# A GEGLU feed-forward kernel: the last float32r product of its down stage as seven block products of 256 columns

## The chip, the cores and the metric

The kernel runs on one core of a Trainium2 chip. The time is the device time of one execution in microseconds; of three executions of the kernel before, the median was 270.98 us (270.94 to 271.31). Five engines work side by side, each with its own queue of instructions: TensorE (PE in the profile; its weight loads are the row PEld), VectorE (DVE), ScalarE (ACT), GpSimd (POOL) and SyncE (SP). SP, ACT and POOL also start transfers (DMAs). Engines wait for each other through semaphores.

## The reference

The input x has 32 x 32 tokens of width 1024, taken as 1024 rows; the weights are w_gate and w_up (1024 x 3584) and w_down (3584 x 1024), all bfloat16.

```
def _gelu(x):
    return jax.nn.gelu(x, approximate=True)

def reference(x, w_gate, w_up, w_down):
    return (_gelu(x @ w_gate) * (x @ w_up)) @ w_down
```

## The kernel before

**Recording and planning.** Every instruction is recorded with `pr.add` (line 58), which works out what it must wait for from the 256-byte pieces of memory that it reads and writes. An instruction has a wished time `at`; `finish` (line 184) sorts each engine's instructions by it, TensorE excepted, which keeps the order of recording, and `emit` (line 205) issues them, so all instructions of the profile carry line 216. Before that, `arrange` (line 124) replaces the wished times in a window `lo` to `hi` by a plan: it walks through the program with a cost for each instruction (`cost`, line 91) and, on each engine but TensorE and SP, takes the instruction that can start first, urgent ones ahead; `SHIFT` (line 830) moves the urgency of single instructions. The window before is 39 to `base` (about 180 us), so the plan covers the gate and up stage. The order in the down stage is written out by hand through the wished times.

**Gate and up stage (to about 180 us).** 28 slabs of 128 columns of the hidden layer are computed into `hT`, stored transposed: `hT[:, m, n]` has the 128 hidden units of slab m on the partitions and 1024 tokens n in the columns, in bfloat16. From slab pair 3 on (`SECOND`), one of the products of each pair is itself taken as seven block products of 256 columns (`inner`, line 572). In this stage POOL makes part of the weight sums, and one sum of each of nine pairs (`sums_w`, line 468) is made by a ScalarE copy and an adding transfer: a DMA issued by POOL with `accum_op=ADD`, which adds its source to what stands at its destination.

**Down stage.** The product of `hT` (3584 x 1024 tokens) with the down weights `wd` (3584 x 1024 columns) is split in two along tokens (i), hidden units (j) and columns, and the eight half-size products are replaced by seven. Products 1 and 2 are plain bfloat16; products 7, 5, 6, 3 and 4 (in this order) are float32r products of sums of activations and sums of weights. Each of the seven is a `sweep` (line 741): 14 slabs deep, 4 tiles of 128 tokens, 512 columns, so 56 matrix products. VectorE makes the sums in pieces of 1024 columns (`prep7` to `prep4`, lines 774 to 792): activation sums into 20 slots of `S`, weight sums into 16 slots of `T2r`. A slot is used again when TensorE has read it. ScalarE makes plain float32r copies where an operand is no sum (`cs`). PSUM has eight banks, four for each of two groups, `PA` and `PB`; ScalarE copies a finished group into the other where two results begin alike.

Product 4, the last sweep, is the one that the change replaces. Its stationary operand is the activations h11 (slabs 14 to 27, tokens 512 to 1023), copied to float32r by ScalarE (`cs(1, k)`); its moving operand is the weight sum `ws(2, k)`; it is added on top of the sums that stand in `PA`. Two lines set it up, and its results leave through `done4` (line 798), alternately over VectorE and ScalarE:

```
tt(bank(PA[t]), bank(PA[t]), p7[t], ADD, begin[3] + 2.9 + 0.1 * t)
tt(late[:, 0, t, :], bank(PA[t]), p5[t], ADD, begin[3] + 2.9 + 0.1 * t)
...
sweep(4, PA, False, lambda k, t: S[:, c_at(1, k), t * P:(t + 1) * P], one_w(2), done4, prep4)
```

The second of these lines makes four output tiles while product 3 starts, and SP stores them (`out_dma`, line 736). After product 4 TensorE does a bfloat16 rest that was left over from product 2: 14 products of 384 and 14 of 128 columns (line 818), each piece copied out and stored by SP. The rest's PSUM banks are filled from `p1` by ScalarE.

Of the kernel before, what the change touches and what calls it, by code (L numbers as in the profile page):

```python
# [6 lines left out]
P = 128  # L7
# [12 lines left out]
class _Program:  # L20
# [70 lines left out]
    def cost(self, op):  # L91
        name, args, _ = op.call
        ins = [a for a in args[1:] if hasattr(a, "tensor")]
        n = math.prod(args[0].shape[1:])
        if op.eng == "pe":
            wide = ins and ins[-1].dtype == F32R
            step = max(n / 2400 + (0.0133 if wide else 0.0026), 0.112 if wide else 0.056)
            return step, step + 0.165
        if op.sem:
            if name != "dma_start":  # L100
                return 1.25, 6.0
            size = math.prod(args[0].shape) * WIDTH[args[0].dtype] / 1e6
            if op.eng == "pool":
                return (1.5, 3.8 + size / 0.19) if op.call[2] else (1.0, 3.1 + size / 0.3)
# [118 lines left out]
def bass_standalone__geglu_ffn__sampling_kernel(  # L223
# [21 lines left out]
    with ExitStack() as es:  # L245
        def sb(name, shape, dtype):
            return es.enter_context(nc.sbuf_tensor(name, shape, dtype))

        hT = sb("hT", [P, FM, N], BF16)
        arena = sb("arena", [P, 28672], BF16)  # L250
        S = sb("S", [P, 20, 512], F32R)
        T = sb("T", [P, 8, 4, 2, P], F32R)
# [12 lines left out]
        pr.alias = {tqr.name: (tmp[:, :, :].tensor.name, 8192), p1r.name: (p1[:, :].tensor.name, 0)}  # L265
# [25 lines left out]
        def tt(out, a, b, op, at, eng="dve", after=()):  # L291
            return pr.add(eng, "tensor_tensor", out, a, b, op, at=at, after=after)
# [4 lines left out]
        def dma(eng, out, a, at, name, after=()):  # L297
            return pr.add(eng, "dma_start", out, a, at=at, dma=name, after=after)
# [413 lines left out]
        def wb(i, j, k): return wd[i][j][:, k:k + 2, :]  # L712


        s_at = lambda b, k: 2 * ((b * 7 + k // 2) % 10) + k % 2
        t_at = lambda b, k: 2 * ((b * 7 + k // 2) % 8) + k % 2
        c_at = lambda b, k: 2 + 2 * ((b * 7 + k // 2) % 3) + k % 2
        hs = lambda b, k: S[:, s_at(b, k):s_at(b, k) + 2, :]
        hsf = lambda b, k: Sf[:, s_at(b, k):s_at(b, k) + 2, :]
        ws = lambda b, k: T2r[:, t_at(b, k):t_at(b, k) + 2, :]  # L720
        wsf = lambda b, k: T2f[:, t_at(b, k):t_at(b, k) + 2, :]
        cs = lambda b, k: S[:, c_at(b, k):c_at(b, k) + 2, :]
# [4 lines left out]
        late = arena[:, 0:6144].rearrange("p (o t n) -> p o t n", o=3, n=512)  # L727
        F, H = 0.2266, 0.216
        begin = {}
        now = base  # L730
        for n in (1, 2, 7, 5, 6, 3, 4):
            begin[n] = now
            now += (3 if n == 2 else 4) * NK * (H if n < 3 else F)
        end = now + NK * H

        def out_dma(i, t, j, src):
            dma("sp", out_r[:, 4 * i + t, j * 512:(j + 1) * 512], src, end, "out")

        EDGE = 4

        def sweep(n, banks, start, stat, mov, done, prep=None):


            held = 2 if n == 7 else 3
            steps = [(t, k) for k in range(EDGE) for t in range(4) if t != held] + [(held, k) for k in range(EDGE)]
            steps += [(t, k) for k in range(EDGE, NK - EDGE) for t in range(4)]
            steps += [(t, k) for t in range(4) for k in range(NK - EDGE, NK)]
            if n < 3:
                steps = [(t, k) for t in range(5 - n) for k in range(NK)]
            made = set()  # L750
            for i, (t, k) in enumerate(steps):
                if prep and k // 2 not in made:
                    made.add(k // 2)
                    prep(k)
                mm(banks[t], stat(k, t), mov(k), start and k == 0, k == NK - 1, add=not start)
                if k == NK - 1:
                    done(t, begin[n] + (i + 1) * (H if n < 3 else F))
# [20 lines left out]
        def prep5(k):  # L778
            tt(hs(1, k), hb(1, 0, k), hb(1, 1, k), ADD, clock + V * (14 + k))
            tt(ws(1, k), wb(0, 1, k), wb(0, 0, k), SUB, clock + V * (15 + k))  # L780

        def prep6(k):
            tt(hs(2, k), hsf(1, k), hb(0, 0, k), SUB, clock + V * (28 + k))
            tt(ws(2, k), wb(1, 1, k), wsf(1, k), SUB, clock + V * (29 + k))

        def prep3(k):
            tt(hs(2, k), hb(0, 1, k), hsf(2, k), SUB, max(begin[6] + 4 * F * (k + 3), clock + V * (42 + k / 2)))
            act(cs(0, k), wb(1, 1, k), COPY, begin[3] + 4 * F * (k - 5))

        def prep4(k):  # L790
            tt(ws(2, k), wb(1, 0, k), wsf(2, k), SUB, begin[3] + 3.5 + 4 * F * k)
            act(cs(1, k), hb(1, 1, k), COPY, begin[4] + 4 * F * (k - 5))

        def done3(t, at):
            tt(late[:, 1, t, :], bank(PB[t]), p5[t], ADD, at)
            out_dma(0, t, 1, late[:, 1, t, :])

        def done4(t, at):
            if t % 2 == 0:
                pr.add("dve", "tensor_copy", late[:, 2, t, :], bank(PA[t]), at=at)  # L800
            else:
                act(late[:, 2, t, :], bank(PA[t]), COPY, at)
            out_dma(1, t, 0, late[:, 2, t, :])

        one_t = lambda b: (lambda k, t: S[:, s_at(b, k), t * P:(t + 1) * P])
        one_w = lambda b: (lambda k: T2r[:, t_at(b, k), :])
        sweep(7, PA, True, one_t(0), one_w(0), lambda t, at: act(p7[t], bank(PA[t]), COPY, at), prep7)
        sweep(5, PA, True, one_t(1), one_w(1), lambda t, at: act(p5[t], bank(PA[t]), COPY, at), prep5)
        sweep(6, PB, False, one_t(2), one_w(2), lambda t, at: act(bank(PA[t]), bank(PB[t]), COPY, at), prep6)
# [4 lines left out]
        sweep(3, PB, False, one_t(2), lambda k: S[:, c_at(0, k), :], done3, prep3)  # L814
        sweep(4, PA, False, lambda k, t: S[:, c_at(1, k), t * P:(t + 1) * P], one_w(2), done4, prep4)


        pieces = ((PB[0], 0, 384), (PB[1], 384, 512))
        for b, c0, c1 in pieces:
            act(ps[:, b, 0:c1 - c0], p1[:, c0:c1], COPY, begin[4] + 6)  # L820
        for b, c0, c1 in pieces:
            for k in range(NK):
                mm(b, ht(0, 1, k, 3), wd[1][0][:, k, c0:c1], False, k == NK - 1, add=True)
            if c0 == 0:
                act(o11[:, 3, c0:c1], ps[:, b, 0:c1 - c0], COPY, end)
            else:
                pr.add("dve", "tensor_copy", o11[:, 3, c0:c1], ps[:, b, 0:c1 - c0], at=end)
            dma("sp", out_r[:, 3, c0:c1], o11[:, 3, c0:c1], end, "out")

        SHIFT = {0: {16: 0.4, 22: -1.3},  # L830
                 2: {11: 0.2},
                 11: {7: -0.5},
                 12: {21: 1.8},
                 "steady": {22: 1.7}}
# [5 lines left out]
_INS = ['x', 'w_gate', 'w_up', 'w_down']  # L840
_OUTS = [((32, 32, 1024), 'bfloat16')]
# [23 lines left out]
```

## Time and profile before

| what | value |
|---|---|
| median of three executions | 270.98 us |
| the profiled execution's own time | 270.95 us |
| its span, first to last instruction | 269.3 us |
| TensorE busy | 266.6 us (99%) |
| VectorE busy | 229.4 us (85%) |
| ScalarE busy | 137.4 us (51%) |
| POOL busy | 88.8 us (33%) |
| product 3 starts, product 4 starts, rest starts | 238.82, 251.51, 264.21 us |
| granted TensorE clock | 1.00 throughout |

Times in the profile count from the span's start; around the span lie another 1.65 us of the execution. A row of a group names the source line, the engine, the operation, the written and read tiles with their shape and how often it occurred, then the busy time, the mean duration in ns and the idle time before it with what ended it. A row of a timeline has the start, the time to the end of the last instruction merged into it, and the count. A matrix product's duration includes its drain, which overlaps the next product; the pace is read from the starts. TensorE is busy all the time, so the other engines' busy shares matter only where TensorE would have to wait for them, and the last stores matter because the execution ends when they have landed.

### The profile page before, as it was taken

The numbers are of one execution on the slowest core, as the hardware profiler recorded it, in microseconds if no ns is written. First come the engines' busy times: TensorE is split into PE (matmuls) and PEld (weight loads), VectorE is DVE, ScalarE is ACT, GpSimd is POOL, SyncE is SP. The second block draws the span as 40 slices with busy tenths as digits, with TensorE's granted clock in tenths as the row PEclk, the third lists the DMA queues.
The fourth block names the chain that finished last, engine by engine and source line by source line (L and its number), as shares of the span: only waits on it lengthen the run. The fifth ranks groups of instructions, "written<-read, shape, count | busy, mean of one in ns | idle before, by whom it ended". The sixth has DMA issues, their size and how long they took to land.

```text
span 269.3 us, 3654 instructions
## 1 busy us (share of the span) xinstructions
PE 266.6 (99%) x1272; PEld 193.5 (72%) x1272; DVE 229.4 (85%) x301; ACT 137.4 (51%) x243; POOL 88.8 (33%) x69
## 2 busy tenths in 40 slices
PE   8999999999999999999999999999999999999997
PEld 3444448888888888888586867764458888888884
DVE  1338999999999999999999999599976999999921
ACT  1339877666676576656464755521220305067452
POOL 1000019499798999995524330000000000000000
DMA  6999955995999999998930700492010000002102
GB/s 193 221 349 234 252 157 65 163 242 68 185 217 202 251 224 233 231 251 196 281 127 0 253 22 1 125 353 69 2 39 19 0 0 2 0 1 78 58 22 97
DMA packets 63746, 36.94 MB, mean 137 GB/s; under 512 B 8944, under 2 KB 63728, under 8 KB 63728
## 3 DMA queue, kind: packets, MB, share of 16 engines
q1 hardware_dynamic: 42496, 25.04, 33.0%
q0 software_dynamic: 18720, 9.44, 28.2%
q10 hardware_dynamic: 2512, 2.23, 3.1%
q8 instruction: 10, 0.16, 0.2%
q14 instruction: 8, 0.07, 0.1%
HBM read 23.33 MB, written 2.10 MB: 94 GB/s over the span
## 4 chain that ended last, share of the span: by engine, by line
PE 99%; DVE 0%; issue 0%
PE ps L216 99%; DVE o L216 0%
## 5 line engine op out<-in xcount | busy, mean ns | idle before, releaser
L216 PE MATMUL ps<-S,T 128*128 128x512 f32 (+1 forms) x516 | 120.1, 383 | 0.0
L216 PEld LDWEIGHTS ps<-S,T 128*128 128x128 f32 x516 | 94.6, 188 | 18.6 <-DMA T<-arena 0.2
L216 ACT ACTIVATE tmp<-ps 128x512 f32<-128x512 f32 (+1 forms) x75 | 36.3, 505 | 38.7 <-PE ps L216 37.5
L216 DVE TENSOR_TENSOR T<-arena,T 128x1024 fp32r<-128x1024 bf16 x42 | 54.6, 1308 | 0.1
L216 PE MATMUL ps<-T,S 128*128 128x512 f32 x224 | 51.3, 390 | 0.0
L216 PEld LDWEIGHTS ps<-T,S 128*128 128x128 f32 x224 | 42.1, 188 | 8.8
L216 POOL TENSOR_TENSOR T<-arena 128x1024 fp32r<-128x1024 bf16 x17 | 38.3, 2255 | 21.1 <-PE ps L216 19.2
L216 ACT ACTIVATE ps<-ps 128x512 f32<-128x512 f32 (+1 forms) x55 | 28.9, 537 | 32.0 <-PE ps L216 31.4
L216 PE MATMUL ps<-arena 128*128 128x512 bf16 x192 | 42.6, 381 | 0.0
L216 DVE TENSOR_TENSOR hT<-tmp,ps 128x512 bf16<-128x512 f32 x56 | 37.1, 680 | 5.0 <-PE ps L216 4.1
L216 DVE TENSOR_TENSOR tmp<-ps,tmp 128x256 f32<-128x256 f32 (+1 forms) x72 | 35.4, 522 | 5.6 <-PE ps L216 4.0
L216 PEld LDWEIGHTS ps<-arena 128*128 128x128 bf16 x192 | 17.8, 98 | 23.7 <-ACT ps L216 2.4
L216 ACT ACTIVATE tmp<-tmp 128x512 f32<-128x512 f32 x28 | 17.5, 632 | 21.7 <-DVE tmp L216 21.7
L216 PE MATMUL ps<-arena,hT 128*128 128x512 bf16 (+2 forms) x126 | 24.6, 356 | 0.0
L216 DVE TENSOR_TENSOR ps<-ps,tmp 128x512 f32<-128x512 f32 x32 | 22.2, 696 | 2.6 <-PE ps L216 2.3
L216 POOL DMA_DIRECT2D T<-arena x18 | 22.3, 1434 | 6.2 <-ACT T L216 3.4
L216 DVE TENSOR_TENSOR T<-arena 128x1024 fp32r<-128x1024 bf16 x16 | 19.0, 1220 | 4.0 <-PE ps L216 4.0
L216 PEld LDWEIGHTS ps<-arena,hT 128*128 128x128 bf16 x126 | 11.7, 98 | 12.8 <-issue 0.5
L216 POOL TENSOR_TENSOR tq<-S 128x512 fp32r<-128x512 f32 x2 | 4.2, 2090 | 38.1 <-PE ps L216 38.1
L216 DVE TENSOR_TENSOR S<-hT 128x1024 fp32r<-128x1024 bf16 x14 | 16.6, 1219 | 0.0
L216 ACT ACTIVATE ps<-hT 128x512 f32<-128x512 f32 x22 | 13.0, 596 | 4.5 <-DVE hT L216 2.4
L216 ACT ACTIVATE T<-arena 128x1024 fp32r<-128x1024 bf16 x14 | 14.8, 1059 | 0.4
(50 smaller groups left out, 200.3 us busy)
## 6 DMA issues: line engine op xcount, KB each, us to landing
T<-arena POOLq DMA_DIRECT2D x18, 512.0 KB, 6.7
arena<-in_w_down_dram SPq DMA_DIRECT2D x4, 1792.0 KB, 9.0
arena<-in_w_gate_dram SPq DMA_DIRECT2D x10, 512.0 KB, 4.0
arena<-in_w_up_dram SPq DMA_DIRECT2D x10, 512.0 KB, 5.3
out_dram<-arena SPq DMA_DIRECT2D x12, 128.0 KB, 1.7
arena<-in_w_up_dram ACTq DMA_DIRECT2D x6, 128.0 KB, 5.3
arena<-in_w_gate_dram SPq DMA_DIRECT2D x3, 256.0 KB, 5.6
arena<-in_w_up_dram SPq DMA_DIRECT2D x3, 256.0 KB, 5.9
```

The lines of the kernel that those rows point to most:

```text
L216: ins = name(eng, *args, **kw) if callable(name) else getattr(eng, name)(*args, **kw)
```

## The change

Product 4 is itself split in two along tokens, depth and columns, and computed as seven block products: each has 7 depths, 2 tiles of 128 tokens and 256 columns, 98 matrix products in all. The depth is split by even and odd slabs (h11, h12, h21, h22 of `rows` are views of `hT`).

- Activations: a11, a12 and a22 are float32r copies by ScalarE. The four sums s1 = h21 + h22, s2 = s1 - h11, s3 = h11 - h21 and s4 = h12 - s2 are made by a ScalarE copy or negation followed by an adding transfer from POOL (`plus`). s4 needs s2 first, and s2 needs s1. They lie in `wr`, memory that held the down weights wd[0][0] and wd[0][1]; a11, a12 and more lie over the front of `hT` (`hr`, `hf`).
- Weights: four sets of differences by VectorE (`sums_b`), each in a part of 5 and a part of 2 depths, 1280 and 512 columns. The last set is written over weights that an earlier block reads.
- Results: blocks that begin alike are copied between PSUM banks by ScalarE (256 columns); VectorE joins blocks with `u3` (the sum of what stood in `PA` and product 7) in 256-column additions.
- The four output tiles that were made at the start of product 3 are now made among the last block results and stored by POOL (queue name `side`) rather than SP; SP waits for both at the end.
- Slots: activation and weight sums sit at other places, four pairs of weight sums of product 5 in `spare`, a view of `tmp`; all sums of product 5 are recorded ahead of its sweep.
- `arrange` now covers the down stage too (`end + 20` in place of `base`), with another `SHIFT`, and the plan's cost of a POOL transfer has one more rate. By the order of the instructions that results, VectorE has 18 more than before, ScalarE 2 more, POOL 8 more, SP 4 fewer and TensorE 42 more; in the gate and up stage only a few neighbours on ScalarE and VectorE change places.

```
+        hr = nc.alloc_sbuf_tensor_at("hr", [P, FM, 512], F32R, offset=at_h)
+        hf = nc.alloc_sbuf_tensor_at("hf", [P, FM, 512], FP32, offset=at_h)
+        wr = nc.alloc_sbuf_tensor_at("wr", [P, 4, 7, 256], F32R, offset=at_w)
...
-            out_dma(0, t, 0, o11[:, t, :])
+            out_dma(0, t, 0, o11[:, t, :], "out" if t else "early")
...
+        def negate(o, a, at):
+            pr.add("act", "activation", o, a, COPY, at=at, scale=-1.0)
...
-        def prep4(k):
-            tt(ws(2, k), wb(1, 0, k), wsf(2, k), SUB, begin[3] + 3.5 + 4 * F * k)
-            act(cs(1, k), hb(1, 1, k), COPY, begin[4] + 4 * F * (k - 5))
...
-        for t in range(4):
-            tt(bank(PA[t]), bank(PA[t]), p7[t], ADD, begin[3] + 2.9 + 0.1 * t)
-            tt(late[:, 0, t, :], bank(PA[t]), p5[t], ADD, begin[3] + 2.9 + 0.1 * t)
-            out_dma(1, t, 1, late[:, 0, t, :])
-        sweep(4, PA, False, lambda k, t: S[:, c_at(1, k), t * P:(t + 1) * P], one_w(2), done4, prep4)
...
+        rows = [hT[:, 14 + i:28:2, 512 + r * 256:768 + r * 256] for r in range(2) for i in range(2)]
+        h11, h12, h21, h22 = rows
+        a11, a12, a22 = hr[:, 0:7, 0:256], hr[:, 7:14, 0:256], flat(8192)
+        s1, s2, s3, s4_ = (wr[:, i] for i in range(4))
+
+        def plus(o, a, name, after=()):
+            pr.add("pool", "dma_start", o, a, at=begin[6] + 6, dma=name, after=after, accum_op=ADD)
+
+        act(s1, h21, COPY, begin[6])
+        plus(s1, h22, "sa")
+        negate(s2, hT[:, 14:28:2, 512:768], begin[6] + 1)
+        plus(s2, s1.bitcast(FP32), "sb")
+        negate(s3, h21, begin[6] + 2)
+        plus(s3, h11, "sc")
+        negate(s4_, s2.bitcast(FP32), begin[6] + 4)
+        plus(s4_, h12, "sd")
+
+        u3 = p7
+        for t in range(4):
+            tt(u3[t], bank(PA[t]), p7[t], ADD, begin[3] + 2.9 + 0.1 * t)
...
+        act(a11, h11, COPY, begin[3])
+        act(a12, h12, COPY, begin[3] + 1)
+        act(a22, h22, COPY, begin[4])
...
+        def sums_b(out, p, q):
+            for k0, k1 in ((0, 5), (5, 7)):
+                tt(out(k0, k1), p(k0, k1).bitcast(FP32), q(k0, k1).bitcast(FP32), SUB, begin[3] + 6)
+        B = lambda i, c: (lambda k0, k1: b(i, c, k0, k1))
+        T1 = lambda k0, k1: hr[:, k0:k1, 256:512]
+        T2_ = lambda k0, k1: flat(6144)[:, k0:k1, :]
+        sums_b(T1, B(0, 1), B(0, 0))
+        sums_b(T2_, B(1, 1), T1)
+        sums_b(B(0, 1), B(1, 1), B(0, 1))
+
+        def block(bk, l, r, start, t):
+            for k in range(7):
+                pr.add("pe", "matmul", ps[:, bk, 0:256], l[:, k, t * P:(t + 1) * P], r(k, k + 1)[:, 0, :],
+                       start=start and k == 0, stop=k == 6, skip_group_check=not start)
+
+        for t in range(2):
+            block(q0[t], a11, B(0, 0), True, t)
+            act(q(q1[t]), q(q0[t]), COPY, begin[4])
+        for t in range(2):
+            block(q5[t], s1, T1, True, t)
+            tt(r5[2 + t], q(q5[t]), u3[2 + t][:, R], ADD, begin[4])
+            tt(r5[t], q(q5[t]), u3[t][:, R], ADD, begin[4])
+        for t in range(2):
+            block(q1[t], s2, T2_, False, t)
+            act(q(q5[t]), q(q1[t]), COPY, begin[4])
+        for t in range(2):
+            block(q0[t], a12, B(1, 0), False, t)
+            tt(done4(t)[:, L], q(q0[t]), u3[t][:, L], ADD, begin[4])
+        sums_b(B(1, 0), B(1, 0), T2_)
+        for t in range(4):
+            tt(late(t), u3[t], p5[t], ADD, begin[4], after=pr.ops["dve"][-1:])
+            out_dma(1, t, 1, late(t), "side", "pool")
+        for t in range(2):
+            block(q5[t], s3, B(0, 1), False, t)
+            tt(done4(2 + t)[:, R], q(q5[t]), r5[2 + t], ADD, begin[4])
+        for t in range(2):
+            block(q1[t], s4_, B(1, 1), False, t)
+            tt(done4(t)[:, R], q(q1[t]), r5[t], ADD, begin[4])
+            out_dma(1, t, 0, done4(t))
+        for t in range(2):
+            block(q5[t], a22, B(1, 0), False, t)
+            tt(done4(2 + t)[:, L], q(q5[t]), u3[2 + t][:, L], ADD, begin[4])
+            out_dma(1, 2 + t, 0, done4(2 + t))
...
-        pr.arrange(39, base, range(4, 9), SHIFT)
+        pr.arrange(39, end + 20, range(4, 9), SHIFT)
...
-            pr.emit(e, eng, sems, [("out", totals["out"])] if e == "sp" else ())
+            pr.emit(e, eng, sems, [(n, totals[n]) for n in ("out", "side")] if e == "sp" else ())
```

More of the change, by code (lines that the diff above doesn't have):

```diff
@@ L103, in cost @@
             if op.eng == "pool":
-                return (1.5, 3.8 + size / 0.19) if op.call[2] else (1.0, 3.1 + size / 0.3)
+                rate = 0.25 if args[0].shape[-1] > 256 else 0.19 if op.call[2] else 0.3
+                return (1.5, 3.8 + size / rate) if op.call[2] else (1.0, 3.1 + size / rate)
             return 0.62, 2.6 + size / 0.25
@@ L247, in sb @@
             return es.enter_context(nc.sbuf_tensor(name, shape, dtype))
+        at_h = (nc.sbuf_base + 31) // 32 * 32
         hT = sb("hT", [P, FM, N], BF16)
+        at_w = (nc.sbuf_base + 31) // 32 * 32
+        assert at_w == at_h + 57344
         arena = sb("arena", [P, 28672], BF16)
@@ L264, in bass_standalone__geglu_ffn__sampling_kernel @@
         p1r = nc.alloc_sbuf_tensor_at("pq", [P, 2, 2, P], F32R, offset=at_p1)
-        pr.alias = {tqr.name: (tmp[:, :, :].tensor.name, 8192), p1r.name: (p1[:, :].tensor.name, 0)}
+        hr = nc.alloc_sbuf_tensor_at("hr", [P, FM, 512], F32R, offset=at_h)
+        hf = nc.alloc_sbuf_tensor_at("hf", [P, FM, 512], FP32, offset=at_h)
+        wr = nc.alloc_sbuf_tensor_at("wr", [P, 4, 7, 256], F32R, offset=at_w)
+        pr.alias = {hr.name: (hT[:, :, :].tensor.name, 0), hf.name: (hT[:, :, :].tensor.name, 0), wr.name: (arena[:, :].tensor.name, 0), tqr.name: (tmp[:, :, :].tensor.name, 8192), p1r.name: (p1[:, :].tensor.name, 0)}
         ps = es.enter_context(nc.psum_tensor("ps", [P, 8, 512], FP32))
@@ L712, in wb, with wsn @@
         def wb(i, j, k): return wd[i][j][:, k:k + 2, :]
-        s_at = lambda b, k: 2 * ((b * 7 + k // 2) % 10) + k % 2
-        t_at = lambda b, k: 2 * ((b * 7 + k // 2) % 8) + k % 2
-        c_at = lambda b, k: 2 + 2 * ((b * 7 + k // 2) % 3) + k % 2
+        s_at = lambda b, k: 2 * ((0, 7, 14, 14 if k < 8 else 7)[b] + k // 2) % 20 + k % 2
+        c_at = lambda k: 2 * (8, 9, 0)[k // 2 % 3] + k % 2
         hs = lambda b, k: S[:, s_at(b, k):s_at(b, k) + 2, :]
         hsf = lambda b, k: Sf[:, s_at(b, k):s_at(b, k) + 2, :]
-        ws = lambda b, k: T2r[:, t_at(b, k):t_at(b, k) + 2, :]
-        wsf = lambda b, k: T2f[:, t_at(b, k):t_at(b, k) + 2, :]
-        cs = lambda b, k: S[:, c_at(b, k):c_at(b, k) + 2, :]
+        cs = lambda k: S[:, c_at(k):c_at(k) + 2, :]
+        spare = tqr[:, :, :, :].rearrange("p u k n -> p (u k n)").rearrange("p (s n) -> p s n", n=512)
+        def wsn(b, k, n):
+            if b == 1 and 2 <= k < 6:
+                return spare[:, k - 2:k - 2 + n, :]
+            a = 10 + k if b == 1 and k < 2 else 2 * ((6, 3, 2, 1)[b] + k // 2) % 16 + k % 2
+            return T2r[:, a:a + n, :]
+        ws = lambda b, k: wsn(b, k, 2)
+        wsf = lambda b, k: wsn(b, k, 2).bitcast(FP32)
         PA, PB = (0, 1, 2, 3), (4, 5, 6, 7)
@@ L726, in bass_standalone__geglu_ffn__sampling_kernel @@
         p5 = [tmp[:, 4 + t, :] for t in range(4)]
-        late = arena[:, 0:6144].rearrange("p (o t n) -> p o t n", o=3, n=512)
-        F, H = 0.2266, 0.216
+        late = lambda n: hT[:, 7 + n, 512:1024] if n < 7 else o11[:, 0, :]
+        F, H, G = 0.2266, 0.216, 0.12
         begin = {}
@@ L732, in bass_standalone__geglu_ffn__sampling_kernel, with out_dma @@
             begin[n] = now
-            now += (3 if n == 2 else 4) * NK * (H if n < 3 else F)
+            now += (3 if n == 2 else 4) * NK * (H if n < 3 else F) if n != 4 else 14 * 7 * G
         end = now + NK * H
-        def out_dma(i, t, j, src):
-            dma("sp", out_r[:, 4 * i + t, j * 512:(j + 1) * 512], src, end, "out")
+        def out_dma(i, t, j, src, name="out", eng="sp"):
+            dma(eng, out_r[:, 4 * i + t, j * 512:(j + 1) * 512], src, end, name)
         EDGE = 4
         def sweep(n, banks, start, stat, mov, done, prep=None):
+            pr.marks[pr.count] = 20 + n
             held = 2 if n == 7 else 3
@@ L780, in prep5, with sum6 @@
             tt(ws(1, k), wb(0, 1, k), wb(0, 0, k), SUB, clock + V * (15 + k))
+        def sum6(k):
+            tt(ws(2, k), wb(1, 1, k), wsf(1, k), SUB, clock + V * (29 + k))
         def prep6(k):
             tt(hs(2, k), hsf(1, k), hb(0, 0, k), SUB, clock + V * (28 + k))
-            tt(ws(2, k), wb(1, 1, k), wsf(1, k), SUB, clock + V * (29 + k))
+            if not 2 <= k < 6:
+                sum6(k)
         def prep3(k):
-            tt(hs(2, k), hb(0, 1, k), hsf(2, k), SUB, max(begin[6] + 4 * F * (k + 3), clock + V * (42 + k / 2)))
@@ L788, in prep3 @@
-            act(cs(0, k), wb(1, 1, k), COPY, begin[3] + 4 * F * (k - 5))
-        def prep4(k):
-            tt(ws(2, k), wb(1, 0, k), wsf(2, k), SUB, begin[3] + 3.5 + 4 * F * k)
-            act(cs(1, k), hb(1, 1, k), COPY, begin[4] + 4 * F * (k - 5))
-        def done3(t, at):
[L795 to L800, printed above, removed]
-            else:
-                act(late[:, 2, t, :], bank(PA[t]), COPY, at)
-            out_dma(1, t, 0, late[:, 2, t, :])
@@ L805, in bass_standalone__geglu_ffn__sampling_kernel @@
[L805 to L809, printed above, removed]
-        for t in range(4):
-            tt(bank(PA[t]), bank(PA[t]), p7[t], ADD, begin[3] + 2.9 + 0.1 * t)
-            tt(late[:, 0, t, :], bank(PA[t]), p5[t], ADD, begin[3] + 2.9 + 0.1 * t)
-            out_dma(1, t, 1, late[:, 0, t, :])
@@ L814, in bass_standalone__geglu_ffn__sampling_kernel @@
-        sweep(3, PB, False, one_t(2), lambda k: S[:, c_at(0, k), :], done3, prep3)
-        sweep(4, PA, False, lambda k, t: S[:, c_at(1, k), t * P:(t + 1) * P], one_w(2), done4, prep4)
[L818 to L827, printed above, removed]
-            dma("sp", out_r[:, 3, c0:c1], o11[:, 3, c0:c1], end, "out")
@@ L830, in bass_standalone__geglu_ffn__sampling_kernel @@
[L830 to L834, printed above, removed]
-        pr.arrange(39, base, range(4, 9), SHIFT)
+            act(cs(k), wb(1, 1, k), COPY, begin[3] + 4 * F * (k - 5))
+        def done3(t, at):
+            tt(late(4 + t), bank(PB[t]), p5[t], ADD, at)
+            out_dma(0, t, 1, late(4 + t))
+        one_t = lambda b: (lambda k, t: S[:, s_at(b, k), t * P:(t + 1) * P])
@@ new lines, in bass_standalone__geglu_ffn__sampling_kernel @@
+        one_w = lambda b: (lambda k: wsn(b, k, 1)[:, 0, :])
+        sweep(7, PA, True, one_t(0), one_w(0), lambda t, at: act(p7[t], bank(PA[t]), COPY, at), prep7)
+        for k in range(0, NK, 2):
+            prep5(k)
+        for k in (2, 4):
+            sum6(k)
+        sweep(5, PA, True, one_t(1), one_w(1), lambda t, at: act(p5[t], bank(PA[t]), COPY, at))
+        sweep(6, PB, False, one_t(2), one_w(2), lambda t, at: act(bank(PA[t]), bank(PB[t]), COPY, at), prep6)
+        rows = [hT[:, 14 + i:28:2, 512 + r * 256:768 + r * 256] for r in range(2) for i in range(2)]
@@ new lines, in bass_standalone__geglu_ffn__sampling_kernel @@
+        plus(s2, s1.bitcast(FP32), "sb")
[6 more added lines that the diff above has]
+            tt(u3[t], bank(PA[t]), p7[t], ADD, begin[3] + 2.9 + 0.1 * t)
+        pr.marks[pr.count] = 30
+        for k in (8, 10, 12, 0, 2, 4, 6):
+            tt(hs(3, k), hb(0, 1, k), hsf(2, k), SUB, clock + V * 42)
+        for k in range(0, NK, 2):
+            tt(ws(3, k), wb(1, 0, k), wsf(2, k), SUB, begin[3] + 0.01 * k)
@@ new lines, in bass_standalone__geglu_ffn__sampling_kernel, with b @@
+        sweep(3, PB, False, one_t(3), lambda k: S[:, c_at(k), :], done3, prep3)
+        act(a11, h11, COPY, begin[3])
+        act(a12, h12, COPY, begin[3] + 1)
+        act(a22, h22, COPY, begin[4])
+        pr.marks[pr.count] = 31
+        def b(i, c, k0, k1):
+            v = wsn(3, 2 * k0, 2 * (k1 - k0)).rearrange("p (k i) n -> p k i n", i=2)
+            return v[:, :, i, c * 256:(c + 1) * 256]
+        def sums_b(out, p, q):
+            for k0, k1 in ((0, 5), (5, 7)):
+                tt(out(k0, k1), p(k0, k1).bitcast(FP32), q(k0, k1).bitcast(FP32), SUB, begin[3] + 6)
@@ new lines, in bass_standalone__geglu_ffn__sampling_kernel @@
+        q0, q1, q5 = (PA[0], PA[1]), (PB[0], PB[1]), (PA[2], PA[3])
+        q = lambda bk: ps[:, bk, 0:256]
+        done4 = lambda t: arena[:, t * 512:(t + 1) * 512]
+        r5 = [hf[:, i, 0:256] for i in range(4)]
+        L, R = slice(0, 256), slice(256, 512)
+        for t in range(2):
[5 more added lines that the diff above has]
+            tt(r5[t], q(q5[t]), u3[t][:, R], ADD, begin[4])
@@ new lines, in bass_standalone__geglu_ffn__sampling_kernel @@
+        for t in range(2):
[6 more added lines that the diff above has]
+            out_dma(1, 2 + t, 0, done4(2 + t))
+        pieces = ((PB[2], 0, 384), (PB[3], 384, 512))
+        for b_, c0, c1 in pieces:
+            act(ps[:, b_, 0:c1 - c0], p1[:, c0:c1], COPY, begin[4] + 6)
@@ new lines, in bass_standalone__geglu_ffn__sampling_kernel @@
+        for b_, c0, c1 in pieces:
+            for k in range(NK):
+                mm(b_, ht(0, 1, k, 3), wd[1][0][:, k, c0:c1], False, k == NK - 1, add=True)
+            if c0 == 0:
+                act(o11[:, 3, c0:c1], ps[:, b_, 0:c1 - c0], COPY, end)
+            else:
+                pr.add("dve", "tensor_copy", o11[:, 3, c0:c1], ps[:, b_, 0:c1 - c0], at=end)
+            dma("sp", out_r[:, 3, c0:c1], o11[:, 3, c0:c1], end, "out")
+        SHIFT = {0: {11: -0.3, 16: 0.4, 22: -1.3},
+                 23: {9: 0.9},
+                 "steady": {2: 0.8}}
```

1 line of the change is left out of this document (added).

## The prediction, made before the result was known

> **What bounds the kernel now.** I read the page's busy shares and its chain first, then the waits of TensorE.
>
> ```profile
> span 269.3 us, 3654 instructions
> ...
> PE 266.6 (99%) x1272; PEld 193.5 (72%) x1272; DVE 229.4 (85%) x301; ACT 137.4 (51%) x243; POOL 88.8 (33%) x69
> ...
> PE 99%; DVE 0%; issue 0%
> ```
>
> ```profile
> PE ps L216 <- PEq L850: 0.8, 1, 0.8
> ```
>
> TensorE is the whole chain, and the second fence is the only wait it has: 0.8 us at the very start. So TensorE work that disappears is time that disappears, as long as nothing new makes TensorE wait and nothing new ends after it. The timeline of TensorE gives the prices. Its first column is a start, so the differences between rows give the pace; the second column also holds the drain of the last product.
>
> ```profile
> 172.65 0.40 PE L216 MATMUL ps<-tq,pq 128*128 128x256 f32 x2
> 172.89 0.40 PE L216 MATMUL ps<-tq,T 128*128 128x256 f32 x2
> 173.13 1.09 PE L216 MATMUL ps<-S,T 128*128 128x512 f32 x4
> 174.06 0.40 PE L216 MATMUL ps<-tq,pq 128*128 128x256 f32 x2
> ...
> 174.76 0.40 PE L216 MATMUL ps<-tq,T 128*128 128x256 f32 x2
> 175.00 4.72 PE L216 MATMUL ps<-S,T 128*128 128x512 f32 x20
> ...
> 238.82 12.86 PE L216 MATMUL ps<-S 128*128 128x512 f32 x56
> 251.51 12.85 PE L216 MATMUL ps<-T,S 128*128 128x512 f32 x56
> 264.21 3.23 PE L216 MATMUL ps<-arena,hT 128*128 128x384 bf16 x28
> ```
>
> The row at 251.51 is product 4, which the change replaces; the row at 238.82 is product 3; the last is the bf16 rest that closes the kernel. Off the chain, VectorE in the down stage and the transfers:
>
> ```profile
> 200.00:210.00 10.00, 6.04 (x7) 1.00 0.04 13
> 210.00:250.00 40.00, 39.64 (x39) 1.00 0.04 14
> 250.00:262.00 12.00, 6.91 (x9) 1.00 0.13 45
> ```
>
> ```profile
> T<-arena POOLq DMA_DIRECT2D x18, 512.0 KB, 6.7
> ...
> out_dram<-arena SPq DMA_DIRECT2D x12, 128.0 KB, 1.7
> ```
>
> The windows show VectorE alone (length, busy time, clock 1.00, DMA share, GB/s): full from 210 to 250, with 9.4 us free between 200 and 262. The transfer rows end with the us from issue to landing.
>
> **TensorE.** Removed: 56 products of 512 columns, 264.21 - 251.51 = 12.70 us (0.2268 each). Added: 7 blocks x 2 token tiles x 7 depths = 98 float32r products of 256 columns. Twelve such products took (173.13 - 172.65) + (175.00 - 174.06) = 1.42 us, 0.1183 each; so 98 x 0.1183 = 11.59 us and the gain is 1.11 us. Ends: at 0.1200 (the four from 172.65) it is 0.94; at half of a 512 (0.1134) it is 1.59. The longest run in the trace is about eight; 98 in a row are not shown, and I take the mean of both runs.
>
> The weight load of such a product lasts 189 ns in its group, longer than the 118 ns from one product to the next, so loads already overlap. [...]
>
> **VectorE.** Added: four sets of weight differences of 1280 + 512 columns; a 1024-column sum comes every 1.135 us in the timeline (216.68, 217.82, 218.95), so 4 x 1.99 = 8.0 us; 12 additions of 256 columns at 0.33 = 4.0 us. Gone: two 512-column casts, 1.2 us. Net +10.8 us on the engine that is full in these stages, so the deadlines matter. From about 204, where it waits for a slot (the free time of the first window), 29 sums of 1.135 us follow in its new order, to 236.9; then six weight sums of product 4 with four additions from PSUM (0.61 each) to 246.2, the large part of set 1 (1.42) to 247.6, the seventh weight sum to 248.8, the large part of set 2 to 250.2, the small part of set 1 (0.57) to 250.7, two results of product 3, the small part of set 2 to 252.5, set 3 to 254.5, and four 256-column additions and two results to about 257.1. TensorE starts the seven blocks at 251.5, 253.2, 254.8, 256.5, 258.1, 259.8 and 261.4, 14 x 0.1183 = 1.66 us apart. Block 2 reads set 1 (2.5 us early), block 3 set 2 (2.3), block 5 set 3 (3.6). Set 4 overwrites weights that block 4 reads, so it can start only after 258.1 plus the drain: 1.42, one addition of 0.33 and 0.57 end at about 260.8, against 261.4 to 262.0, where block 7 reads its two parts. That cover, 1.2 us or more, is the thinnest of VectorE's; what goes beyond it goes to TensorE one for one. So: zero.
>
> **ScalarE.** Seven 1024-column copies and two casts go (7 x 0.95 + 2 x 0.5 = 7.7 us); seven 1792-column copies (1.66 each from the 1024 row, 11.6 us) and four 256-column copies between banks (0.26 each) come. It is 51% busy; the copies between banks have a whole block, 1.66 us, before their bank is read again. Zero, with one condition: the fourth activation sum is begun by ScalarE from the second, so its negation waits for a transfer in ScalarE's queue, ahead of the copies that product 3 needs (weights from 235.2, banks from 236.1).
>
> **POOL and the adding transfers.** POOL had nothing after 160 us; now four adding transfers and four output stores. The wait for their sources costs nothing behind it but those. The transfers write 0.92 MB each where the trace has 0.52 MB in 6.3 to 9.1 us. Bounds: 6.3, as if size cost nothing, and 9.1 x 1.75 = 15.9. I take 9.5: 2.1 us to the first packet and 4.2 us of packets x 1.75. ScalarE's first copy overwrites down weights that VectorE's second sum after 204 reads, so it runs from 206.3 to 208.0: the first transfer lands at 217.6, the second, which reads the first, at 227.1; ScalarE is free for it from 226.6. The negation and one copy (3.3 us) stand before the copies for product 3, so nothing is late until the second lands after about 232; the fourth sum lands near 238, its reader starts at 259.8. Zero, with the upper end as a rival.
>
> **The end.** SP keeps its last stores. Four stores move from SP, where they left at 242 to 246, to POOL, and their additions (512 columns from SBUF, 0.61 us) move to the end of VectorE's queue, among the block results: 1.42 + 0.57 + 4 x 0.61 + 6 x 0.33 from 258.2, plus short waits: the fourth is ready at 264.3. The chain of the bf16 rest ends at 269.3 - 1.1 = 268.2, so a store must land within 3.9 us. Bounds: 1.7 (SP's 128 KB) and 6.7 (POOL's 512 KB of small packets). In the trace's packets SP's store lands 0.87 us after its first packet, which comes 0.83 us from issue; POOL's first packet comes at 2.13; 2.13 + 0.87 = 3.0, taken because bytes and packets are those of SP's store. It lands at 267.3, hidden by 0.9 us.
>
> The gate and up stage keeps its work. Neighbours swap on ScalarE (0.26 us copies), and two activation sums of product 7 move up into the last pair on VectorE, which is busy 6.5 of the 10 us from 170 to 180: a shift of 1.1 us lies in that idle time. Zero, with the last rival as its price.
>
> **Sum.** 12.70 - 11.59 = 1.11 us out of the profiled execution's 270.95 us (span 269.3 and 1.65 around it): 269.84; the median of before is 270.98, 0.03 above. I predict 269.9 us.
>
> **Rivals.**
> - Stores end last. POOL's queue, not TensorE, sets the end if the fourth lands later than 3.9 us after its source. At 6.7 it lands at 271.0, 1.7 us after the old end: 272.7. If POOL takes 1.56 us to issue each (the longest issue in the trace), from 261.5, the fourth leaves at 266.2 and lands at 269.2: 270.9. For it: these are the last instructions of a queue, and the price is borrowed. Against: issues in pairs stand 0.91 to 1.24 us apart. 17%: 8 still faster, 6 same, 3 slower.
> [...]
> - The adding transfers hold ScalarE. Each us that the second lands after 232 to 233 is a us that product 3 waits. At 15.9 each it lands at 239.8: about 7 us lost, 277. It decides from 12.3 us each. For: 1.75 times the bytes. Against: no transfer in the trace reached 9.2. 10%: 9 slower, 1 same.
> - Weight loads don't overlap over 98 products: at 0.130 each the gain is gone (270.9); at 189 ns it is +5.8, 276.8. Against: eight in succession at 0.1175. 5%: 2 same, 3 slower.
> - VectorE or a slot is late and takes 0.3 to 3 us: 270 to 273. 10%: 3 faster, 3 same, 4 slower.
>
> **Numbers.** The forecast has 58%, its own range 269.3 to 270.2. Faster by over 0.2% (0.54 us, about what a measurement of this kernel tells from none): 58 + 8 + 3 = 69%; same 12%; slower 19%. The range from 269.3 (0.1134) to 271.2 leaves out about 18, nearly all above.
>
> **What would show it.** TensorE's timeline: 98 products of 256 columns in 11.6 us, the bf16 rest starting near 263.1, no wait but the first 0.8. The adding transfers land in 7 to 12 us. The last landing is SP's. A row of TensorE waiting for ScalarE near 239, for VectorE near 262, or POOL's stores as the last event would prove me wrong.

## The result, and the profile after

The changed kernel takes 269.86 us (median of 9 runs, 269.37 to 270.51) against 270.63 us before (9 runs); the ratio is 0.9966, with a 95% interval from 0.9954 to 0.9978. A second comparison on another occasion gave 269.59 against 270.96 us, 0.9943 (0.9924 to 0.9963). So it is faster, by 0.8 and by 1.4 us; 269.9 had been predicted. The profiles below account for 0.94 us. The first interval, 0.6 to 1.2 us, holds that figure; the second, 1.0 to 2.1 us, just leaves it out, and no run shows what the rest is.

The page of the changed kernel, the lines that answer to those of before:

```profile
span 268.7 us, 3748 instructions
...
PE 264.7 (99%) x1305; PEld 194.7 (72%) x1314; DVE 239.9 (89%) x319; ACT 142.0 (53%) x245; POOL 97.4 (36%) x77
...
PE 91%; DMA 4%; DVE 2%; ACT 1%; issue 1%; POOL 0%; ACTq 0%
```

VectorE has 10.5 us more (10.8 was the sum), ScalarE 4.6, POOL 8.6. The chain that ended last now leaves TensorE three times, all before 168 us: at 4.2 us for VectorE, from 65 to 80.5 us through ScalarE, VectorE, POOL and a transfer of 9.7 us (the DMA 4%), and from 163 to 167.7 us for VectorE and ScalarE. TensorE's waits are these; the first, at the start, is in the kernel before too:

```profile
PE ps L217 <- PEq L943: 0.8, 1, 0.8
PE ps L217 <- DMA T<-arena: 0.4, 1, 0.4
PE ps L217 <- DVE arena L217: 0.3, 1, 0.3
```

None of them lies in the down stage: of the two others, the 0.3 us are at 4.8 us, and the 0.4 us at 80.5 us, on an adding transfer of the gate and up stage that is in both kernels. TensorE's timeline at the end, where each row of 14 is one block and the row of 28 at 258.53 is two:

```profile
251.82 1.83 PE L217 MATMUL ps<-T,hr 128*128 128x256 f32 x14
253.49 1.84 PE L217 MATMUL ps<-hr,wr 128*128 128x256 f32 x14
255.17 1.84 PE L217 MATMUL ps<-S,wr 128*128 128x256 f32 x14
256.85 1.84 PE L217 MATMUL ps<-T,hr 128*128 128x256 f32 x14
258.53 3.52 PE L217 MATMUL ps<-T,wr 128*128 128x256 f32 x28
261.89 1.84 PE L217 MATMUL ps<-T,S 128*128 128x256 f32 x14
263.58 3.23 PE L217 MATMUL ps<-arena,hT 128*128 128x384 bf16 x28
```

The seven blocks last 263.58 - 251.82 = 11.76 us, 0.1200 a product, where product 4 lasted 12.70: 0.94 us gained, with no gap inside. That the span shrank by 0.6 only, from 269.3 to 268.7, is because the blocks begin 0.31 us later than product 4 did (251.82 against 251.51): TensorE was 0.26 us ahead after the first 6 us, and from the wait at 80.5 us on it was 0.3 us behind.

The new transfers (us to landing last) and the start of POOL's:

```profile
wr<-hT POOLq DMA_DIRECT2D x3, 896.0 KB, 7.7
wr<-wr POOLq DMA_DIRECT2D x1, 896.0 KB, 8.4
out_dram<-hT POOLq DMA_DIRECT2D x4, 128.0 KB, 2.2
```

```profile
209.18 3.48 POOL L217 DMA_DIRECT2D wr<-hT  x2 [51.79 <-DVE T L217]
217.20 0.90 POOL L217 DMA_DIRECT2D wr<-wr  x1 [4.54 <-DMA wr<-hT]
229.24 1.74 POOL L217 DMA_DIRECT2D wr<-hT  x1 [11.13 <-ACT wr L217]
```

The second sum lands at 217.20 + 8.4 = 225.6 us, ScalarE begins its negation at 227.1, when it has done its other work, and has no copy for product 3 to make until 235.8.

### The profile page after: what moved, and what is told of

Its sections match the earlier page's. It is cut to its first block, busy times and chain, and to the rows that moved or that the text cites. A ratio compares the mean times of both kernels' runs of the same rounds, so it can differ in the third digit from the quotient of the medians.

```text
span 268.7 us, 3748 instructions
## 1 busy us (share of the span) xinstructions
PE 264.7 (99%) x1305; PEld 194.7 (72%) x1314; DVE 239.9 (89%) x319; ACT 142.0 (53%) x245; POOL 97.4 (36%) x77
## 4 chain that ended last, share of the span: by engine, by line
PE 91%; DMA 4%; DVE 2%; ACT 1%; issue 1%; POOL 0%; ACTq 0%
PE ps L217 91%; DMA T<-arena 4%; ACT tmp L217 1%; DVE tmp L217 1%; POOL T L217 0%; ACT T L217 0%; DVE ps L217 0%; DVE hT L217 0%; ACT ps L217 0%; DVE arena L217 0%; DVE o L217 0%; ACTq L215 0%
## 5 line engine op out<-in xcount | busy, mean ns | idle before, releaser
L217 DVE TENSOR_TENSOR T<-arena,T 128x1024 fp32r<-128x1024 bf16 x40 | 52.4, 1313 | 0.2 <-POOL T L217 0.2
L217 ACT ACTIVATE ps<-ps 128x512 f32<-128x512 f32 (+1 forms) x59 | 30.6, 527 | 27.3 <-PE ps L217 26.8
L217 PE MATMUL ps<-arena 128*128 128x512 bf16 x186 | 41.3, 379 | 0.7 <-DVE arena L217 0.3
L217 DVE TENSOR_TENSOR tmp<-ps,tmp 128x256 f32<-128x256 f32 (+1 forms) x76 | 38.2, 530 | 3.5 <-PE ps L217 1.8
L217 PE MATMUL ps<-T,S 128*128 128x512 f32 (+1 forms) x166 | 37.0, 381 | 0.0
L217 PEld LDWEIGHTS ps<-T,S 128*128 128x128 f32 x166 | 30.3, 188 | 6.0
L217 POOL DMA_DIRECT2D wr<-hT x3 | 5.2, 1867 | 62.9 <-DVE T L217 51.8
L217 DVE TENSOR_TENSOR ps<-ps,tmp 128x512 f32<-128x512 f32 x28 | 19.4, 696 | 2.5 <-PE ps L217 1.9
L217 DVE TENSOR_TENSOR T<-arena 128x1024 fp32r<-128x1024 bf16 x14 | 16.9, 1216 | 0.0
```

What stands on the lines that cost most here:

```text
L217: ins = name(eng, *args, **kw) if callable(name) else getattr(eng, name)(*args, **kw)
```

## The experiments

**The plan alone.** The kernel before, with the planned window over the down stage and nothing else:

```
-        pr.arrange(39, base, range(4, 9), SHIFT)
+        pr.arrange(39, end + 20, range(4, 9), SHIFT)
```

> The kernel before with one edit: the planned window also covers the down stage, as in the changed kernel; product 4 stays undivided. Theory (the gain is TensorE's columns alone, and no engine's order in the down stage is on its path): same as before, 270.6 us within 0.3, no wait of TensorE in the down stage. Rival (the new order of the other engines gives part of the 0.8 us): 270.0 to 270.3 us. Rival (the hand order was needed): slower, over 271.

Measured: 271.06 us against 270.85 before, ratio 1.0013 (0.9996 to 1.0031). Product 4 lasts 12.70 us again (251.04 to 263.74), with no wait of TensorE there. Planning the down stage gives no gain by itself, as expected, so the 0.94 us belong to the blocks. (The order that this run gets is the plan's for an undivided product 4, not the order of the changed kernel.)

**The activation sums by VectorE.** The changed kernel, without the adding transfers and the ScalarE copies that begin them:

```
-        act(s1, h21, COPY, begin[6])
-        plus(s1, h22, "sa")
...
+        tt(s1, h21, h22, ADD, begin[6])
+        tt(s2, s1.bitcast(FP32), h11, SUB, begin[6] + 1)
+        tt(s3, h11, h21, SUB, begin[6] + 2)
+        tt(s4_, h12, s2.bitcast(FP32), SUB, begin[6] + 4)
```

> The changed kernel with one edit: the four activation sums of the seven blocks are made by VectorE directly (four subtractions or additions of 1792 columns) in place of a ScalarE copy and an adding transfer each. Theory: that adds 4 x 1792 x 1.135 / 1024 = 7.9 us to VectorE, which has 3 us free from 201 to 204 and at most 1.6 us of cover at the blocks; TensorE then waits for it in the blocks, 3 to 6 us in all, 273 to 276 us, and the change would be a loss without the transfers. Rival (VectorE had room): 269.9 us, same as the changed kernel.

Measured: 277.25 us, ratio 1.0233 to before (1.021 to 1.0256), 7.4 us above the changed kernel and more than the 3 to 6 expected. TensorE's timeline, with its idle time and who ended it in brackets:

```profile
254.28 1.84 PE L217 MATMUL ps<-hr,wr 128*128 128x256 f32 x14
257.18 1.99 PE L217 MATMUL ps<-S,wr 128*128 128x256 f32 x14 [1.06 <-DVE hT L217]
...
262.38 0.82 PE L217 MATMUL ps<-T,wr 128*128 128x256 f32 x5 [1.54 <-ACT ps L217]
264.36 0.50 PE L217 MATMUL ps<-T,wr 128*128 128x256 f32 x2 [1.16 <-DVE T L217]
265.49 4.26 PE L217 MATMUL ps<-T,wr 128*128 128x256 f32 x21 [0.63 <-ACT ps L217]
```

The blocks last 18.64 us (252.61 to 271.25) in place of 11.76. Of the 6.9 us more, 4.4 are waits in these brackets, within the 3 to 6 expected. Another 1.55 are a lower clock (0.57 from 266 to 270 us, next experiment): the 21 products from 265.49 took 4.07 us to the next row, where 0.1200 each would be 2.52. Most of the last 0.9 is the drain ahead of each wait, which the brackets don't count as idle: four times 0.16 us, as a block without a wait behind it lasts 1.84 us and the next starts after 1.68. ScalarE appears as the one that ends two waits, but its bank copies had themselves waited for VectorE's additions that read the same banks:

```profile
261.86 0.37 ACT L217 ACTIVATE ps<-ps 128x256 f32<-128x256 f32 x1 [4.23 <-DVE hf L217]
265.06 0.37 ACT L217 ACTIVATE ps<-ps 128x256 f32<-128x256 f32 x1 [2.83 <-DVE hf L217]
```

So, in this order of work, the blocks pay only because the sums are made off VectorE.

**The fourth set of weight differences held back.** One late addition of 512 columns is repeated, six and then three times, behind the last product of block 4 and ahead of the fourth set:

```
+        hold = pr.ops["pe"][-1:]
+        for i in range(6):
+            hold = [tt(late(3), u3[3], p5[3], ADD, begin[4], after=hold)]
```

> The changed kernel with one edit: before the fourth set of weight differences VectorE repeats one late addition of 512 columns six times, behind the last product of block 4. Theory (the fourth set is ready 1.6 us before block 7 reads its second part, and its delay goes one for one to TensorE beyond that): six times 0.61 to 0.73 us is 3.7 to 4.4, TensorE waits for VectorE at block 7 for 2.0 to 3.2 us, 271.9 to 273.1. Rival (block 7 is not bound to this set, or the cover is larger): under 1 us.

> As the run with six repeats ahead of the fourth set, with three. Six made TensorE wait 3.0 us, and after that wait its granted clock was 0.51 for 3.2 us, which cost another 1.4 us. Each repeat took 0.72 us, so three take 2.2 and the cover takes 1.3 to 1.6 of it: TensorE waits 0.6 to 1.0 us. Theory A (the clock falls after a wait only when the wait is long): clock 1.00, block 7 lasts 1.69 us, 0.6 to 1.0 us above the changed kernel in the span from the first block to the end. Theory B (any wait of this size lowers the clock): block 7 lasts over 2.5 us.

Measured, one execution each: 274.08 us with six (271.9 to 273.1 expected), 271.69 with three. TensorE's rows at block 7 and its rest, six first:

```profile
264.34 3.36 PE L217 MATMUL ps<-T,S 128*128 128x256 f32 x14 [3.00 <-DVE T L217]
267.50 3.38 PE L217 MATMUL ps<-arena,hT 128*128 128x384 bf16 x28
```

```profile
262.88 1.94 PE L217 MATMUL ps<-T,S 128*128 128x256 f32 x14 [0.82 <-DVE T L217]
264.67 3.23 PE L217 MATMUL ps<-arena,hT 128*128 128x384 bf16 x28
```

With three, block 7 starts 0.98 us late and lasts 1.79 us, near its usual 1.69. With six it waits 3.0 us and then lasts 3.16 us: its products come 0.226 us apart in the mean (3.16 / 14). The windows of the run with six, whose columns are length, busy time of PE, PEld, DVE, ACT and POOL, granted clock, DMA share and GB/s, show why:

```profile
255.00:261.00 6.00, 6.00 (x52) 6.00 (x52) 5.29 (x12) 1.33 (x4) 0.00 (x0) 1.00 0.13 45
261.00:264.30 3.30, 0.34 (x3) 0.14 (x2) 3.20 (x5) 0.00 (x0) 0.00 (x0) 1.00 0.00 0
264.30:267.50 3.20, 3.16 (x14) 3.06 (x15) 3.20 (x7) 0.00 (x0) 1.06 (x2) 0.51 0.12 41
267.50:271.00 3.50, 3.38 (x29) 2.21 (x28) 1.54 (x5) 0.49 (x1) 1.21 (x3) 0.96 0.77 262
```

After 3.3 us with 0.34 us of work the granted clock is 0.51 for the next 3.2 us and 0.96 over the 3.5 after those. The blocks took 267.50 - 251.11 = 16.39 us, 4.6 more than usual, for a wait of 3.0: 3.16 with the drain, and 1.47 because block 7 lasted 3.16 in place of 1.69. With three repeats the clock stays 1.00 after the wait of 0.82 us, so of the two theories of that run the figures of A came, not those of B. VectorE's fourth set of differences (1280 and 512 columns), in the changed kernel and then with three repeats, shows what block 7 waits for:

```profile
258.50 1.49 DVE L217 TENSOR_TENSOR T<-T,S 128x1280 fp32r<-128x1280 f32 x1 [0.17 <-PE ps L217]
260.24 0.68 DVE L217 TENSOR_TENSOR T<-T,S 128x512 fp32r<-128x512 f32 x1
```

```profile
261.35 2.09 DVE L217 TENSOR_TENSOR T<-T,S 128x1280 fp32r<-128x1280 f32 x2
```

In the changed kernel the first part is ready at 259.99 for a read at 261.89 and the second at 260.92 for a read five products later, at 262.49: 1.9 and 1.6 us of cover. With the repeats the two parts stand back to back, and block 7 starts when the first ends. In the run before this one, with the sums on VectorE, TensorE was busy 3.78 us of the six from 256 to 262 and 1.84 of the four to 266, and the clock was 0.57 from 266 to 270 and 1.00 from there: ahead of that stood four waits of 1.06, 1.54, 1.16 and 0.63 us. So the low clock came after one wait of 3.0 us and after these four, and did not come after one of 0.82 us; where between them it sets in was not tried.

**The second adding transfer in steps.** s2 += s1 is made in two or four transfers, each waiting for the one before. The plan stays the same but for one place: ScalarE's negation now stands ahead of the last of four copies out of PSUM (0.5 us) instead of behind it:

```
-        plus(s2, s1.bitcast(FP32), "sb")
+        more = ()
+        for i, (k0, k1) in enumerate(((0, 2), (2, 4), (4, 5), (5, 7))):
+            plus(s2[:, k0:k1], s1[:, k0:k1].bitcast(FP32), ("sb", "sx", "sy", "sz")[i], more)
+            more = pr.ops["pool"][-1:]
```

> The changed kernel with one edit: the second adding transfer (s2 += s1) is made in two steps, each waiting for the one before; the order of every other engine is kept. Theory (ScalarE's queue has cover until the second sum lands near 232, where it landed at 225.6): it now lands at 228 to 231, and nothing moves, 269.9 us within 0.6. Rival (no cover): the time grows by 3 to 5 us.

> As the two steps, with four steps in succession. Theory: each takes 4.5 to 5 us, so the second sum lands at 235 to 237; ScalarE's negation stands in front of the copies for product 3, TensorE waits near 239 to 242 for ScalarE, and the time grows by what the landing exceeds 232.7, 2.5 to 4.5 us, to 272 to 274. Rival (the negation has more cover than I worked out, or TensorE is not held by ScalarE there): no change.

Measured, one execution each: 269.65 us with two steps, 270.44 with four (before beside them 271.08). The steps were quicker than I had set (four from 217.4 to 233.5 us, 4.0 each, where 4.5 to 5 had been taken), so the second sum landed at 227.7 with two (228 to 231 expected) and at 233.5 with four (235 to 237 expected; 2.5 to 4.5 us of loss had followed from that). ScalarE with four:

```profile
233.52 1.72 ACT L221 ACTIVATE wr<-wr 128x1792 fp32r<-128x1792 f32 x1 [7.01 <-DMA wr<-wr]
...
237.20 1.06 ACT L221 ACTIVATE S<-arena 128x1024 fp32r<-128x1024 bf16 x1
```

Its queue stood 7.0 us behind the landing, and the first copy for product 3 started at 237.2 in place of 235.8. TensorE lost 0.3 us in product 3, counted product by product against the changed kernel, and one of its weight loads there waits for ScalarE (0.28 us ahead of a later one are put down to VectorE):

```profile
239.76 0.76 PEld L221 LDWEIGHTS ps<-S 128*128 128x128 f32 x4 [0.27 <-ACT ps L221]
```

So the mechanism is there, the point from which it costs is a landing near 233, in one execution, and the changed kernel is 7 us away from it. That a later landing costs one for one beyond this was not tried.

**The four stores on SP's queue.**

```
-            out_dma(1, t, 1, late(t), "side", "pool")
+            out_dma(1, t, 1, late(t))
```

> The changed kernel with one edit: the four late output tiles are stored by SP's queue again, not by POOL's. My theory (TensorE's columns alone make the gain, and POOL's stores are hidden because the fourth landed 1.4 us before the last event, 267.25 against 268.69): nothing moves, 269.9 us within 0.3, the last landing is still the bf16 rest's. Rival (a POOL store at the very end costs something outside the span or delays the engines): 269.3 us or less. A second rival (SP's queue, in order, now waits for the fourth tile ahead of the block results' stores): the end moves by up to 0.5 us to 270.4.

Measured: 270.11 us, ratio 0.998 to before (0.9966 to 0.9994); beside 0.9966 for the changed kernel the intervals overlap. The profile shows what the number cannot. SP's queue at the end, with the stores on SP and then in the changed kernel:

```profile
261.31 3.13 SPq L217 DMA_DIRECT2D out_dram<-hT  x4
264.49 1.91 SPq L217 DMA_DIRECT2D out_dram<-arena  x4
266.44 0.94 SPq L217 DMA_DIRECT2D out_dram<-o  x2
```

```profile
263.15 2.69 SPq L217 DMA_DIRECT2D out_dram<-arena  x4
266.58 0.92 SPq L217 DMA_DIRECT2D out_dram<-o  x2
```

With all ten on SP the block results' stores wait behind the fourth late tile, and from 264.5 on SP issues one every 0.49 us without a pause until the end. From the first product of the rest to the span's end it takes 5.57 us (263.01 to 268.58) where the changed kernel takes 5.13. So the second rival of that run holds in the profiles, one against one, by 0.44 us.

**The weight loads of the gate and up stage issued later.** The wait at 80.5 us is for the second of a pair of POOL transfers; SP issues two 512 KB loads beside them. The edit, in the changed kernel and, as a control, in the kernel before:

```
-            for q, g, s in ((1, 2, 1), (3, 3, 1), (5, 4, 1), ...):
+            for q, g, s in ((1, 2, 1), (5, 4, 1), ...):
...
                 product(7, 1, C[1], False)
+                mid = pr.ops["pe"][-1]
...
+            if p == 3:
+                load_duo(3, 1, t0, after=[mid])
```

> The changed kernel with one edit in the gate and up stage: the two 512 KB weight loads that SP issues at 70.0 and 70.4 us, beside a pair of POOL transfers (69.3 and 70.8), are issued about 4 us later, behind a later product of the same pair. Theory: the loads share the transfer engines with the pair, whose second transfer therefore lands 9.7 us after issue in place of 6.7, and TensorE waits 0.4 us for it at 80.5 us. With the loads later the second transfer lands in 7 to 8 us, TensorE's only wait after the start goes, and the time is 0.4 to 0.6 us below the changed kernel, 269.3 us, with less spread. Rival (the wait is chance of one execution): no change, 269.9 us. Other rival (the loads are now late for POOL's weight sum near 83 us): slower by up to 1 us.

Measured: 269.27 us, ratio 0.9948 to before (0.9933 to 0.9963), 0.6 us below the changed kernel's 269.86. As that set had no run of the changed kernel, three kernels were compared on one chip:

> The changed kernel itself, beside the two others of this set on one chip. The blocks' saving is 0.94 us in the profiles; the median was 0.77 below before. Expected: 0.6 to 1.0 us below before.

> The changed kernel with the two weight loads issued later, a second time, for a direct comparison. Theory (the loads delay the pair of POOL transfers for which TensorE waits): 0.3 to 0.7 us below the changed kernel of this set, 1.2 to 1.6 us below before. Rival (the earlier difference was the chip's): within 0.2 us of the changed kernel.

> The kernel before with the two weight loads issued later, and nothing else. Theory (the wait for the pair of transfers is in the kernel before too, where the profiled execution missed it by 0.05 us): 0.2 to 0.6 us below before. Rival (only the changed kernel meets that wait, as its TensorE or its other engines run otherwise in the gate and up stage): no change from before.

| kernel | median | ratio to before, 95% interval |
|---|---|---|
| changed | 269.59 us | 0.9943 (0.9924 to 0.9963) |
| changed, loads later | 269.54 us | 0.9940 (0.9921 to 0.9959) |
| before, loads later | 270.91 us | 0.9994 (0.9981 to 1.0007) |

The transfers issued from 68.9 to 71.6 us, in the changed kernel of this set and with the loads later:

```profile
T<-arena POOLq DMA_DIRECT2D x2, 512.0 KB, 9.6
arena<-in_w_gate_dram SPq DMA_DIRECT2D x1, 512.0 KB, 5.0
arena<-in_w_up_dram SPq DMA_DIRECT2D x1, 512.0 KB, 9.4
```

```profile
T<-arena POOLq DMA_DIRECT2D x2, 512.0 KB, 6.6
```

The loads do delay the pair, by 3 us, and TensorE's wait (0.7 us in this profile of the changed kernel) is gone when they come later; but the medians differ by 0.05 us, where 0.3 to 0.7 had been expected, and the kernel before gains 0.05 us where 0.2 to 0.6 had been expected. The 0.6 us that the first set seemed to show did not come again. With the loads beside, the pair landed 8.6 to 9.6 us after issue in five profiled executions (before, changed twice, plan alone, stores on SP); of all ten with them, TensorE didn't wait for it in seven and waited 0.2, 0.4 and 0.7 us in three. The changed kernel itself came out 1.4 us below before in this set, more than the 0.6 to 1.0 expected. That the wait explains the changed kernel's spread of 1.1 us is not shown, and this version is not shown to be better.

## Why the prediction was right, step by step

- **The number.** That 269.86 lies beside 269.9 is partly luck. The forecast took 1.08 us off a median of 270.98; beside the changed kernel the one before took 270.63, 0.35 less, and the gain was 0.77. Two misses cancelled. In the second comparison the gain was 1.37, larger than forecast.
- **TensorE.** Right in kind, and a sixth too large: 0.1183 us a product had been taken, the mean of a run of four at 0.1200 and of eight at 0.1175; all 98 came at 0.1200. The gain is 0.94, the lower end given, not 1.11. The fear that weight loads would not overlap over 98 products is refuted: a load lasts 192 ns in the blocks and the products still come 0.1200 us apart. The other end (0.1134) did not come either.
- **VectorE.** The sum of its work and the deadlines held: the fourth set was ready at 260.9 us (260.8 in the working, with TensorE 0.3 us later), and no wait came. The cover was put at 1.2 us or more and bound at the second part; in the changed kernel it was 1.6 us, and the second part is the thinner one, as the working has it (1.9 for the first). What was wrong is "one for one": nearly true for the 0.8 us wait, which cost 1.1, but the 3.0 us wait cost 4.6, 1.47 of it at the clock of 0.51.
- **ScalarE and the adding transfers.** 9.5 us each had been taken; they landed 7.2 to 8.4 us after issue, one, issued while another was under way, after 10.7. The second sum came at 225.6 in place of 227.1. The condition "nothing late until about 232" agrees to a microsecond with the run in four steps. The upper end of 15.9 was far off: that one apart, the 1.75 times larger transfers took 7.2 to 8.4 us where those of before had taken 6.2 to 9.1.
- **The stores.** 3.0 us had been taken from issue to landing, 2.2 measured; the fourth landed at 267.25, 1.4 us before the end. Three figures of the working do not come out of its rows: the terms for the fourth tile add to 264.6, not 264.3 (five additions stand ahead of it, not six; it was ready at 264.65 with TensorE 0.3 us later), the longest POOL issue of before is 1.69 us, not 1.56, and its pairs stand up to 1.49 us apart, not 1.24. None of them decided anything: POOL issued these stores 0.9 to 1.0 us apart, as VectorE made the tiles. The stores left at 262.2 to 265.0 us, and VectorE was busy for all 2.78 us between the first and the last. The move to POOL had been priced only as a risk; the profile of the run with SP shows that it also saves 0.44 us at the end, which the medians are too coarse to show.
- **The gate and up stage at zero.** The plan-only run, whose order there differs too little to matter, agrees. But the 0.03 us between the profiled execution of before and its median hid that single executions differ in that stage: the blocks begin anywhere from 251.1 to 251.9 us in the profiles of the changed kernel and of three runs that alter only what comes behind their start. So one profile against another shows 0.6 us of the 0.94, and the rest began at 263.58 us, not near 263.1.

## What to carry to other kernels

On a kernel whose first engine never waits, count the matrix columns and the pace that the same shape already has in the trace, and take the slower of two paces for a long run (here 0.1200 us, not 0.1175). Then give every helper's new work a place and a deadline: here the same sums cost nothing as transfers and 7.4 us on the full VectorE. Price a wait on TensorE by what one of that length cost in a run, not by its length: here 3.0 us cost 4.6 and 0.8 us cost 1.1. And a gain of a third of a per cent needs the pace read from the rows: two sets of runs gave 0.8 and 1.4 us for it.

## What the runs showed that was not expected

After a TensorE wait of 3.0 us its granted clock was 0.51 over the next 3.2 us, and after four waits of 0.6 to 1.5 us within ten it was 0.57 over 4 us, while after one of 0.8 us it stayed 1.00. A POOL store of 128 KB landed in 2.2 us, only 0.5 us behind SP's 1.7, so POOL's queue was a cheap place for the four last stores here: 5.13 us from the first product of the rest to the span's end, against 5.57 with all ten on SP. Two 512 KB loads beside a pair of POOL transfers stretched the pair's landing from 6.6 to between 8.6 and 9.6 us.
